# Three casts of q and k moved from GpSimd to ScalarE in a kernel that interleaves sparse attention with a two-layer network

## The chip, the cores and the metric

The kernel runs on one core of a Trainium2 chip. The metric is the device time of one execution in microseconds. The time before is the median of three runs; beside them there is one execution that was recorded by the hardware profiler, and every row of a view comes from that one.

The core's engines each work through their own queue in order: TensorE (PE in the views; its weight loads are PEld), VectorE (DVE), ScalarE (ACT), GpSimd (POOL) and SyncE (SP). A wait at the head of a queue holds everything behind it. SyncE, and in this kernel GpSimd too, issue loads and stores (DMAs).

## The reference

```python
def _attn_ref(q, k, v):                      # 8 batches, 8 heads, 576 positions, 64 wide, float32
    scores = scale * np.matmul(q, k.transpose(0, 1, 3, 2))
    rel = pos[:, None] - pos[None, :]
    mask_local = (rel >= 0) & (rel < 32)                        # heads 0 to 3
    mask_strided = (rel >= 0) & (pos[None, :] % 32 == pos[:, None] % 32)   # heads 4 to 7
    ...                                      # masked softmax over the keys
    return np.matmul(attn, v)

x = attn_out.transpose(0, 2, 1, 3).reshape(B * S, H * D)        # 4608 x 512
h = x @ w_in                                                    # 512 x 2048
g = np.maximum(h, 0.0) + alpha * np.minimum(h, 0.0)
out = g @ w_out                                                 # 2048 x 512
```

## The kernel before

The 4608 rows of x are worked through in nine chunks of 512: a first layer (`hps`, L583), the activation by ScalarE and VectorE (`neg` L591, `gT` L594), and a second layer (`ops`). Attention for a batch's 576 rows must be there before the chunk that uses them, so its pieces are interleaved with the matmuls of the chunk before. Two heads make a pair; a batch has four pairs, two local and two strided. Pair 4 is the first of batch 1, pair 8 the first of batch 2.

For a pair there are these pieces. `T`: q or k of the local heads is transposed by TensorE (L269) and copied from PSUM by ScalarE and VectorE (L207, L209) to `qT` or `kT`. `sc1` and `score_both`: scores by TensorE (L353), exponentials by ScalarE (L367 and L371, in later batches L376 and L382), and a multiplication by the mask, on VectorE for batch 1 (L373) and on GpSimd afterwards (L378, L385). `Pv`: the weighted sum of v (L406), a reciprocal (L413) and the normalisation (L415), both by VectorE. `X`: the result is transposed (L429) and copied to `xT`.

The local q and k of a batch come in as float32 (`load_qk`, L104; tiles `ql`, `kl`) and are cast to float16 by `cast_l` ahead of the transposition. `cast_copy` (L205 to L211) picks the engine: `act` is ScalarE (L207), `dve` VectorE (L209), anything else GpSimd (L211). A cast is one instruction over 128 partitions and 1152 elements. v is loaded by `load_v` (L189, L199) and the strided q and k by `load_d` (L134); GpSimd issues these, and the loads of q and k for batches 1 and 2, and those of `w_out` (L739).

All functions that issue instructions are bound to program order on their engine, so the order in the lists is the order in the queues. The change lies in the list that is run between the first chunk's first layer and the second chunk's. In it `U(kf)` is a step of the first chunk's second layer for three row blocks (three matmuls, L866), `W(i)` two steps for the fourth (L881), `vs` a cast of the strided v by VectorE, `ov` a copy of v's overlapping rows (L209), `G` a transposition of the strided q or k. `loads2` issues the six loads of batch 2 from GpSimd; in the kernel before it also casts batch 2's q and k there. At its end, `U(15)` has its three results copied out by ScalarE, VectorE and ScalarE, which frees the three PSUM banks (`hps`) that the second chunk's first layer uses. After the list come two casts of batch 2's strided v on GpSimd and, on SyncE, the transposing DMAs of its strided q and k and the loads for batch 3.

PSUM banks of the kind `ps`, used by T, Pv, X and parts of the scores, are three, taken in turn: a piece waits until the reader of the third piece before it is done.

Of the kernel before, what the change touches and what calls it, by code (L numbers as in the profile page):

```python
# [32 lines left out]
def kernel(  # L33
# [63 lines left out]
    def load_qk(b, nm):  # L97

        src = q if nm == "q" else k
        t32 = hpool.tile([128, 2, 576], F32, tag=f"{nm}l", bufs=2, name=f"{nm}l")  # L100
        loaded[(b, False, nm)] = t32
        base = src[b, 0:1, 0:1, :]
        eng = nc.gpsimd if b in (1, 2) else nc.sync
        keep(eng.dma_start(t32, bass.AP(  # L104
            tensor=base.tensor, offset=base.offset,
            ap=[[9 * D, 64], [2 * S * D, 2], [S * D, 2], [1, 9 * D]])))
# [24 lines left out]
    def load_d(b):  # L131

        for nm, src in (("q", q), ("k", k)):
            keep(nc.gpsimd.dma_start(  # L134
                qks[nm][0:72], src[b, 4:8, :, :].rearrange("h (p t) d -> p h (t d)", t=8)))
# [24 lines left out]
    def turn_second(nm, pr, eng):  # L160

        dst = (qTs if nm == "q" else kTs)[1].rearrange("r e c -> r (e c)")
        tp = pspool.tile([128, 1024], F16, tag="ps", name="tf")
        for j in range(8):
            keep(nc.tensor.transpose(
                tp[:, 72 * j : 72 * j + 72],
                qks[nm][0:72, 2 * pr + j // 4, 128 * (j % 4) : 128 * (j % 4) + 128], ident[0:72, 0:72]))
        cast_copy(eng, dst[:, 640 * pr : 640 * pr + 640].rearrange("r (j p) -> r j p", p=80)[:, :, 0:72],
                  tp[:, 0:576].rearrange("r (j p) -> r j p", p=72))
# [7 lines left out]
    def cast_l(b, nm, eng="pool"):  # L177
        t16 = hpool.tile([128, 9, 2, 64], F16, tag=f"{nm}l16", bufs=2, name=f"{nm}l16")
        cast_copy(eng, t16, loaded[(b, False, nm)].rearrange("p f (t d) -> p t f d", t=9))
        cast16[(b, False, nm)] = t16  # L180
# [24 lines left out]
    def cast_copy(eng, o, i):  # L205
        if eng == "act":
            keep(nc.scalar.copy(o, i))  # L207
        elif eng == "dve":
            keep(nc.vector.tensor_copy(o, i))  # L209
        else:  # L210
            keep(nc.gpsimd.tensor_copy(o, i))  # L211

    def cast_v(b, pr, eng):

        v16 = vss[b % 2]
        cast_copy(eng, v16[0:72, 2 * pr : 2 * pr + 2, :, 0:64],
                  loaded[b][0:72, 1024 * pr : 1024 * pr + 1024].rearrange(
                      "p (h t d) -> p h t d", h=2, t=8))
        cast16[(b, True, "v")] = v16
# [170 lines left out]
    def pv_piece(P, a):  # L390
        while defer and any(P.et[z][0] is defer_et["et"] for z in P.et):
            defer.pop(0)()
        if P.x16 is None:
            if P.xd and P.strided:
                P.x16 = x16s
            else:
                P.x16 = xpool.tile([128, 1024], F16, tag="x16", name="x16")
        v16 = cast16[(P.b, P.strided, "v")]
        grp = P.pgroups[a]
        r = 72 if P.strided else 128  # L400
        pv = pspool.tile([128, 512], F32, tag="ps", name="pv")
        nb = 2 * len(grp)
        for x in range(nb):
            t, hh = grp[x // 2], x % 2
            et, c = P.et[(t, hh)]
            keep(nc.tensor.matmul(  # L406
                pv[:, 65 * x : 65 * x + 65], et[0:r, c : c + 128],
                v16[0:r, 2 * P.pr + hh, t, :] if P.strided else v16[:, 6 * (2 * P.pr + hh) + t, :],
                start=(x == 0), stop=(x == nb - 1), skip_group_check=True))
        w = P.w  # L410
        rc = rpool.tile([128, 8], F32, tag="rc", name="rc")
        pvv = pv[0:w, 0 : 65 * nb].rearrange("r (c e) -> r c e", e=65)
        keep(nc.vector.reciprocal(rc[0:w, 0:nb], pvv[:, :, 64]))  # L413
        c0 = 128 * grp[0]
        keep(nc.vector.tensor_tensor(  # L415
            P.x16[0:w, c0 : c0 + 64 * nb].rearrange("r (c e) -> r c e", e=64),
            pvv[:, :, 0:64],
            rc[0:w, 0:nb].unsqueeze(2).to_broadcast([w, nb, 64]), op=ALU.mult))
# [7 lines left out]
    def x_piece(P, eng):  # L426
        xp = pspool.tile([128, 1024], F16, tag="ps", name="xp")
        for t in range(P.n):
            keep(nc.tensor.transpose(  # L429
                xp[:, P.w * t : P.w * t + P.w], P.x16[0 : P.w, 128 * t : 128 * t + 128], ident[0 : P.w, 0 : P.w]))  # L430
        for s0, d0, w in spans(P.b):
            o = xT[:, P.hp, d0 : d0 + w]
            if P.strided:
                cast_copy(
                    eng, o.rearrange("r (p t) -> r p t", t=8),
                    xp[:, 0:576].rearrange("r (t p) -> r p t", t=8)[:, s0 // 8 : (s0 + w) // 8, :])
            else:
                cast_copy(eng, o, xp[:, s0 : s0 + w])
# [24 lines left out]
    def T(u, nm):  # L463
        return lambda: transpose_piece(u, nm)
# [4 lines left out]
    def Pv(g, i):  # L469
        return lambda: pv_piece(pairs[g], i)  # L470

    def X(g, eng=None):
        return lambda: x_piece(pairs[g], eng or ("act" if pairs[g].strided else "dve"))
# [332 lines left out]
    def vs(b, pr):  # L806
        return lambda: cast_v(b, pr, "dve")

    def Cl(b, nm):
        return lambda: cast_l(b, nm)  # L810

    def ov(b, eng, c0, c1):
        return lambda: over_v(b, eng, c0, c1)
# [7 lines left out]
    def G(nm, pr):  # L821
        return lambda: turn_second(nm, pr, "act" if nm == "q" else "dve")

    warm(17)
    for fn in [
        F("q", 0), w(1), F("k", 0), w(1), F("k", 1), Sc(2, 0), vs(0, 0), w(1), F("q", 1), Sc(2, 1), alpha, Pv(2, 0),
        Sc(3, 1), vs(0, 1), Cl(0, "q"), Cl(0, "k"), Pv(2, 2), Sc(3, 0), w(1), Pv(3, 2), T(0, "q"), Pv(3, 0), w(1),
        Pv(3, 1), w(1), T(0, "k"), X(3), w(1), Sc(0, 1), Pv(2, 1), Sc(0, 0), Sc(1, 1), ov(0, "dve", 12, 24),
        ov(0, "pool", 0, 12), Pv(0, 1), X(2), Pv(0, 0), Sc(1, 0), Pv(1, 1), L(1), X(0, "act"), Pv(1, 0), L(2), L(3),
        X(1), L(0)]:  # L830
        fn()
# [18 lines left out]
    def loads2():  # L850
        load_qk(2, "q")
        load_qk(2, "k")
        load_v(2, False)
        load_d(2)
        load_v(2, True)
        cast_l(2, "q")
        cast_l(2, "k")

    banks = []

    def U(kf):
        def run():
            if kf == 0:
                banks.extend(phpool.tile([128, 512], F32, tag="hps", name="ops") for _ in range(3))
            for mt in range(3):
                keep(nc.tensor.matmul(  # L866
                    banks[mt], gTs[0][:, kf, 128 * mt : 128 * mt + 128], wout16[:, kf, :],
                    start=(kf == 0), stop=(kf == 15)))
            if kf == 15:
                for mt in range(3):  # L870
                    osb = opool.tile([128, 512], F32, tag="osb", name="osb")
                    cast_copy("dve" if mt == 1 else "act", osb, banks[mt])
                    keep(nc.sync.dma_start(out[128 * mt : 128 * mt + 128, :], osb))
        return run

    def W(i):
        def run():
            if i == 0:
                ops_cur["t"] = pspool.tile([128, 512], F32, tag="ps", name="ops")
            for kf in (2 * i, 2 * i + 1):  # L880
                keep(nc.tensor.matmul(  # L881
                    ops_cur["t"], gTs[0][:, kf, 384:512], wout16[:, kf, :], start=(kf == 0), stop=(kf == 15)))
            if i == 7:
                osb = opool.tile([128, 512], F32, tag="osb", name="osb")
                keep(nc.scalar.copy(osb, ops_cur["t"]))
                keep(nc.sync.dma_start(out[384:512, :], osb))
        return run

    def sc1(g):
        return lambda: score_both(pairs[g], "dve")  # L890

    for fn in [
        U(0), Cl(1, "q"), G("k", 1), vs(1, 0), vs(1, 1), sc1(6), U(1), U(2), sc1(7), U(3), U(4), Cl(1, "k"), loads2,
        Pv(6, 0), Pv(7, 0), Pv(6, 2), U(5), Pv(7, 1), U(6), T(2, "q"), Pv(7, 2), U(7), T(2, "k"), Pv(6, 1), U(8),
        X(7, "dve"), W(0), W(1), sc1(4), U(9), W(2), sc1(5), W(3), ov(1, "dve", 0, 24), W(4), U(10), X(6), U(11),
        Pv(4, 1), W(5), Pv(4, 0), U(12), Pv(5, 1), U(13), U(14), Pv(5, 0), U(15), W(6), X(5), X(4), W(7)]:
        fn()
    for pr in range(2):
        cast_v(2, pr, "pool")
# [63 lines left out]
```

## Time and profile before

| | |
|---|---|
| median of three runs | 302.83 us (302.43 to 303.22) |
| the profiled execution | 303.51 us |
| its span, from the first to the last instruction | 301.5 us |
| TensorE busy | 293.3 us, 97% |
| VectorE busy | 220.8 us, 73% |
| ScalarE busy | 175.5 us, 58% |
| GpSimd busy | 175.8 us, 58% |
| granted TensorE clock | 1.00 |

In a timeline a row gives the start in us from the beginning of the span, the duration in us, the engine, the line of the kernel, the operation, what it writes and reads, the shape, and how many instructions the row merges; brackets give the idle time before it and what ended that. A view of groups gives busy time in us and the mean of one instruction in ns, then the idle time before the group. The row of a window gives, in this order, its length and the busy time of PE, PEld, DVE, ACT and POOL. A view of one line gives minimum, median and maximum duration in ns. A busy share is an average over stages, so the stage in question is read by itself.

### The profile page before, as it was taken

Reading aid. Unit: us, or ns where it says so; the run is one execution under the profiler, and the core shown is the slowest. Engines: PE = TensorE matmul, PEld = TensorE weight load, DVE = VectorE, ACT = ScalarE, POOL = GpSimd, SP = SyncE. Lnnn points to the kernel's source line nnn. Section 1 sums busy time; section 2 is a strip of 40 time slices with the busy share of each in tenths; the row PEclk is TensorE's granted clock in tenths of the full one; section 3 lists DMA queues with packets and bytes.
Section 4 is the critical chain, followed back from the end, with each engine's and each line's share of the span. In section 5 each row is a group of like instructions: output and inputs, shape, how many; then the busy total and the mean of one; then the engine's idle time right before and its main releaser. Section 6 shows DMA issues by size and latency. Waiting matters only on the chain.

```text
span 301.5 us, 6823 instructions
## 1 busy us (share of the span) xinstructions
PE 293.3 (97%) x2683; PEld 181.8 (60%) x2683; DVE 220.8 (73%) x408; ACT 175.5 (58%) x327; POOL 175.8 (58%) x163
## 2 busy tenths in 40 slices
PE   7999989999999999999999999999999999999995
PEld 2664545454555468746874687467745964684484
DVE  4677886768775897589848984888489948936852
ACT  1676734398647775676467646764676356516730
POOL 8362264229959998979897988494653405002300
PEclk9999999999999999999999999999999999999999
DMA  7999999999998979899989998955910140022004
GB/s 179 257 193 202 259 180 252 174 185 334 105 209 159 106 105 81 140 198 140 126 166 188 148 140 170 183 92 91 205 24 20 22 142 0 2 72 70 0 2 140
DMA packets 96976, 41.18 MB, mean 137 GB/s; under 512 B 75360, under 2 KB 93232, under 8 KB 96944
## 3 DMA queue, kind: packets, MB, share of 16 engines
q0 software_dynamic: 51008, 17.77, 57.4%
q1 hardware_dynamic: 45584, 22.32, 34.1%
q10 hardware_dynamic: 352, 0.66, 0.9%
q8 instruction: 21, 0.34, 0.5%
q14 instruction: 11, 0.09, 0.1%
HBM read 38.24 MB, written 9.44 MB: 158 GB/s over the span
## 4 chain that ended last, share of the span: by engine, by line
PE 80%; DVE 10%; ACT 4%; issue 3%; DMA 2%; SPq 0%; ACTq 0%; DVEq 0%
PE hps L583 35%; PE ops L708 25%; PE ops L622 5%; PE pv L406 4%; DVE gT L594 3%; PE ops L866 2%; DVE x L415 2%; PE sp L353 2%; DMA consts<-consts 2%; ACT neg L591 2%; DVE gsum L652 2%; PE xp L429 1%; PE sph L353 1%; PE tp L269 1%; PE ops L881 1%
## 5 line engine op out<-in xcount | busy, mean ns | idle before, releaser
L583 PE MATMUL hps<-xT,win 128*128 128x512 f16 x576 | 131.9, 379 | 0.2 <-ACT xT L452 0.2
L594 DVE SCALAR_TENSOR_TENSOR gT<-neg,oma,hps 128x512 f16<-128x512 f32 x144 | 105.3, 744 | 36.4 <-ACT neg L591 28.4
L591 ACT ACTIVATE neg<-hps 128x512 f32<-128x512 f32 x144 | 85.8, 598 | 35.7 <-PE hps L583 33.7
L583 PEld LDWEIGHTS <-win 128*128 128x128 f16 x576 | 53.7, 98 | 59.2 <-issue 0.5
L652 POOL TENSOR_TENSOR gsum<-gT 128x1024 f16<-128x1024 f16 x14 | 29.7, 2124 | 42.2 <-DVE gT L594 37.2
L378 POOL TENSOR_TENSOR et<-et,consts 128x576 f16<-128x576 f16 (+1 forms) x24 | 34.7, 1447 | 31.7 <-ACT et L376 31.5
L708 PEld LDWEIGHTS <-gsum 128*128 128x128 f16 x448 | 40.9, 98 | 7.3 <-DVE gsum L652 1.9
L708 PE MATMUL ops<-wsum,gsum 128*128 128x256 f16 x328 | 41.6, 273 | 0.3
L708 PEld LDWEIGHTS <-gT 128*128 128x128 f16 x336 | 31.5, 98 | 5.4 <-issue 0.3
L415 DVE TENSOR_TENSOR x<-pv,rc 96x384 f16<-96x384 f32 (+2 forms) x62 | 33.0, 532 | 2.1
L385 POOL TENSOR_TENSOR et<-et,consts 128x576 f16<-128x576 f16 (+1 forms) x24 | 31.4, 1310 | 0.0
L406 PEld LDWEIGHTS <-et 72*128 72x128 f16 (+1 forms) x448 | 23.3, 98 | 13.1 <-issue 1.8
L708 PE MATMUL ops<-wout,gT 128*128 128x256 f16 x224 | 27.9, 273 | 0.1
L376 ACT ACTIVATE et<-sp 128x576 f16<-128x576 f32 (+1 forms) x24 | 15.5, 644 | 17.1 <-PE sp L353 17.1
L413 DVE RECIPROCAL rc<-pv 96x6 f32<-96x6 f32 (+2 forms) x80 | 14.6, 183 | 10.4 <-PE pv L406 10.2
L663 DVE TENSOR_TENSOR osb<-ops,par 128x512 f32<-128x512 f32 (+1 forms) x14 | 9.4, 673 | 16.1 <-PE ops L708 8.2
L382 ACT ACTIVATE et<-sph 128x288 f16<-128x288 f32 (+1 forms) x48 | 18.8, 409 | 0.0
L661 ACT COPY osb<-ops 128x512 f32<-128x512 f32 x14 | 8.2, 585 | 16.8 <-PE ops L708 16.7
L406 PE MATMUL pv<-vs,et 72*128 72x65 f16 x256 | 15.4, 193 | 1.7 <-DVE x L415 0.9
L211 POOL COPY vs<-stv 72x1024 f16<-72x1024 f16 x12 | 13.3, 1116 | 6.3 <-DMA stv<-in_v_dram 6.3
L622 PE MATMUL ops<-wout,gT 128*128 128x512 f16 x64 | 16.4, 379 | 0.0
L725 ACT COPY par<-ops 128x512 f32<-128x512 f32 x13 | 7.6, 585 | 14.1 <-PE ops L708 14.1
(103 smaller groups left out, 334.0 us busy)
## 6 DMA issues: line engine op xcount, KB each, us to landing
out_dram<-osb SPq DMA_DIRECT2D x35, 256.0 KB, 3.8
vl<-in_v_dram POOLq DMA_DIRECT2D x6, 384.0 KB, 9.4
win<-in_moe_w_in_dram POOLq DMA_DIRECT2D x4, 512.0 KB, 17.4
wout<-in_moe_w_out_dram POOLq DMA_DIRECT2D x4, 512.0 KB, 17.9
qsd<-in_q_dram POOLq DMA_DIRECT2D x7, 288.0 KB, 5.8
ksd<-in_k_dram POOLq DMA_DIRECT2D x7, 288.0 KB, 7.9
stv<-in_v_dram POOLq DMA_DIRECT2D x7, 288.0 KB, 8.1
ql<-in_q_dram SPq DMA_DIRECT2D x3, 576.0 KB, 6.9
```

The source lines that it names most:

```text
L376: keep(nc.scalar.activation(ev.rearrange("r (y c) -> r y c", y=2), sp[0:r, :, 0:n], AF.Exp, scale=SCALE))
L378: keep(nc.gpsimd.tensor_tensor(mv, mv, m, op=ALU.mult))
L382: keep(nc.scalar.activation(ev[:, n * y : n * y + n], sps[y][0:r, 0:n], AF.Exp, scale=SCALE))
L385: keep(nc.gpsimd.tensor_tensor(mv, mv, m, op=ALU.mult))
L406: keep(nc.tensor.matmul(pv[:, 65 * x : 65 * x + 65], et[0:r, c : c + 128], v16[0:r, 2 * P.pr + hh, t, :] if P.strided else v16[:, 6 * (2 * ...
L415: keep(nc.vector.tensor_tensor(P.x16[0:w, c0 : c0 + 64 * nb].rearrange("r (c e) -> r c e", e=64), pvv[:, :, 0:64], rc[0:w, 0:nb].unsqueeze ...
L583: keep(nc.tensor.matmul(hps, win16[:, kk, 128 * m : 128 * m + 128], xT[:, kk, c0 : c0 + 512], start=(kk == 2), stop=(kk == 1)))
L591: keep(nc.scalar.activation(neg, hps, AF.Relu, scale=-1.0))
L594: keep(nc.vector.scalar_tensor_tensor(gTs[n][:, m, :], neg, oma[:, m : m + 1], hps, op0=ALU.mult, op1=ALU.add))
L622: keep(nc.tensor.matmul(ops, gTs[n][:, kf, 128 * mt : 128 * mt + 128], wout16[:, kf, :], start=(kf == 0), stop=(kf == 15)))
L652: keep((nc.vector if eng == "dve" else nc.gpsimd).tensor_tensor(gsum[i][:, hs], a, b, op=op))
L708: keep(nc.tensor.matmul(o, lhs(y), rhs(y), start=(first and y == 0), stop=(y == 7), skip_group_check=True))
```

## The change

In the list, the cast of batch 1's local k goes to ScalarE and is moved ahead of `U(3)`, behind `sc1(7)`. Batch 2's two casts leave `loads2`, where they followed the six loads on GpSimd, and go to ScalarE too: q behind `Pv(4, 0)`, k behind `U(12)`. The cast of batch 1's local q stays on GpSimd, as do those of batches 0, 3 and 4. The loads and their order are the same.

```diff
-    def Cl(b, nm):
-        return lambda: cast_l(b, nm)
+    def Cl(b, nm, eng="pool"):
+        return lambda: cast_l(b, nm, eng)
...
         load_v(2, False)
         load_d(2)
         load_v(2, True)
-        cast_l(2, "q")
-        cast_l(2, "k")
...
     for fn in [
-        U(0), Cl(1, "q"), G("k", 1), vs(1, 0), vs(1, 1), sc1(6), U(1), U(2), sc1(7), U(3), U(4), Cl(1, "k"), loads2,
+        U(0), Cl(1, "q"), G("k", 1), vs(1, 0), vs(1, 1), sc1(6), U(1), U(2), sc1(7), Cl(1, "k", "act"), U(3), U(4), loads2,
         Pv(6, 0), Pv(7, 0), Pv(6, 2), U(5), Pv(7, 1), U(6), T(2, "q"), Pv(7, 2), U(7), T(2, "k"), Pv(6, 1), U(8),
         X(7, "dve"), W(0), W(1), sc1(4), U(9), W(2), sc1(5), W(3), ov(1, "dve", 0, 24), W(4), U(10), X(6), U(11),
-        Pv(4, 1), W(5), Pv(4, 0), U(12), Pv(5, 1), U(13), U(14), Pv(5, 0), U(15), W(6), X(5), X(4), W(7)]:
+        Pv(4, 1), W(5), Pv(4, 0), Cl(2, "q", "act"), U(12), Cl(2, "k", "act"), Pv(5, 1), U(13), U(14), Pv(5, 0), U(15), W(6), X(5), X(4), W(7)]:
```

## The prediction, made before the changed kernel had run

> **What bounds the kernel now.** I read the page first, then the stage around the change in the timeline of each engine, then the waits and the windows behind it.
>
> ```profile
> span 301.5 us, 6823 instructions
> PE 293.3 (97%) x2683; PEld 181.8 (60%) x2683; DVE 220.8 (73%) x408; ACT 175.5 (58%) x327; POOL 175.8 (58%) x163
> PE 80%; DVE 10%; ACT 4%; issue 3%; DMA 2%; SPq 0%; ACTq 0%; DVEq 0%
> ```
>
> TensorE is busy for 293.3 of 301.5 us, and the chain of waits lies on it for 80%. So the end moves only if time in which TensorE stands still goes or comes. The places to look at are TensorE's gaps while the second batch is prepared: the casts that move all lie between 39 and 55 us. This is TensorE there (start, duration, then in brackets the idle time and who ended it), with one row of the chain of waits at the end:
>
> ```profile
> 41.99 0.81 PE L866 MATMUL ops<-wout,gT 128*128 128x512 f16 x3
> 43.51 0.36 PE L406 MATMUL pv<-vs,et 72*128 72x65 f16 x6 [0.71 <-DVE x L415]
> ...
> 47.09 0.81 PE L866 MATMUL ops<-wout,gT 128*128 128x512 f16 x3
> 52.75 0.82 PE L866 MATMUL ops<-wout,gT 128*128 128x512 f16 x3
> 54.04 0.36 PE L406 MATMUL pv<-vl,et 128*128 128x65 f16 x6 [0.47 <-DVE vl L209]
> 59.19 2.75 PE L583 MATMUL hps<-xT,win 128*128 128x512 f16 x12
> ```
>
> ```profile
> 43.87 0.65 PE ops L866 x3
> ```
>
> Two gaps are ended by VectorE. Three matmuls of L866 take 0.65 us from issue to issue (the chain's row), so what follows the three at 41.99 could have gone at 42.64 and went at 43.51: 0.87 us late. The same reckoning at 52.75 gives 53.40 against 54.04: 0.64 us late. The row's idle figures, 0.71 and 0.47, are smaller since a matmul's recorded 0.81 holds its drain. Why VectorE is late stands in its own timeline and in GpSimd's:
>
> ```profile
> 41.45 1.31 DVE L373 TENSOR_TENSOR et<-et,consts 72x576 f16<-72x576 f16 x1
> 42.90 0.55 DVE L415 TENSOR_TENSOR x<-pv,rc 72x384 f16<-72x384 f32 x1
> ...
> 51.63 0.46 DVE L373 TENSOR_TENSOR et<-et,consts 128x576 f16<-128x576 f16 x1 [0.58 <-ACT et L367]
> 52.24 1.17 DVE L373 TENSOR_TENSOR et<-et,consts 128x576 f16<-128x576 f16 x1
> 53.44 0.54 DVE L209 COPY vl<-vl 32x1495 f16<-32x1495 f16 x1
> ```
>
> ```profile
> L373 DVE TENSOR_TENSOR et<-et,consts x8: 450/458/1309, 38.8 to 52.2; 72x576 f16<-72x576 f16 x4, 128x576 f16<-128x576 f16 x4
> ```
>
> ```profile
> 39.58 1.15 POOL L211 CAST ql<-ql 128x1152 f16<-128x1152 f32 x1 [7.08 <-DMA ql<-in_q_dram]
> 41.31 1.14 POOL L211 CAST kl<-kl 128x1152 f16<-128x1152 f32 x1 [0.58 <-DMA kl<-in_k_dram]
> 42.39 0.71 POOL L104 DMA_DIRECT2D ql<-in_q_dram  x1
> ...
> 51.63 1.47 POOL L211 CAST ql<-ql 128x1152 f16<-128x1152 f32 x1 [4.22 <-DMA ql<-in_q_dram]
> 53.59 1.40 POOL L211 CAST kl<-kl 128x1152 f16<-128x1152 f32 x1 [0.49 <-DMA kl<-in_k_dram]
> 61.30 2.02 POOL L211 COPY vs<-stv 72x1024 f16<-72x1024 f16 x2 [6.31 <-DMA stv<-in_v_dram]
> 67.65 1.27 POOL L378 TENSOR_TENSOR et<-et,consts 128x576 f16<-128x576 f16 x1 [4.33 <-ACT et L376]
> ```
>
> L373 multiplies the exponentials by the mask; both operands lie in SBUF. Six of its eight calls take about 0.458 us, the median. The other two are the ones that start while GpSimd casts: 41.45 falls into the cast of batch 1's k (41.31 to 42.45) and takes 1.31, 52.24 falls into the cast of batch 2's q (51.63 to 53.10) and takes 1.17. Each ends 0.31 us after the cast does. It also works the other way: the cast at 51.63 met the multiplication at 51.63 and took 1.47 instead of 1.14. So a cast on GpSimd and a mask multiplication on VectorE exclude each other for most of their time, and in these two places TensorE pays. These two casts, and that of batch 2's k, are the ones that leave GpSimd.
>
> **The change, part by part.** The sum is made against the profiled execution, 303.51 us (span 301.5 and 2.01 around it).
>
> Cast of batch 1's k away from GpSimd: the call at 41.45 shrinks from 1.31 to 0.46, so VectorE is 0.85 us earlier in a queue that has no gap up to the L415 at 42.90. That L415 frees the PSUM bank for the weighted sum at 43.51; its end moves from 43.45 to 42.60. TensorE can go at 42.64 by its own queue, and with the 0.06 us that lay between the two it goes at 42.66. Gain 0.85.
>
> Cast of batch 2's q away: the call at 52.24 shrinks from 1.17 to 0.46, by 0.71, and the copy of v's overlap rows (L209, 53.44), for which TensorE waits at 54.04, ends 0.71 earlier. TensorE would be let go at 53.33 and gets there at 53.40. Gain 0.64, the whole gap.
>
> Cast of batch 2's k away (53.59, 1.40 us): GpSimd's next instruction waits for a load until 61.30, the one after it at 67.65 for ScalarE. Nobody waits for this cast. Gain 0.
>
> Three casts onto ScalarE. The trace has no such cast from SBUF there. These are the nearest rows, and ScalarE's timeline where they go:
>
> ```profile
> L452 ACT COPY xT<-xs 128x576 f16<-128x576 f16 x4 | 5.3, 1317 | 0.0
> L207 ACT COPY xT<-xp 128x576 f16<-128x576 f16 x8 | 5.1, 641 | 4.8 <-PE xp L429 4.8
> L452 ACT COPY xT<-xs 128x192 f16<-128x192 f16 x2 | 1.2, 577 | 0.0
> L207 ACT COPY xT<-xp 128x192 f16<-128x192 f16 x2 | 0.7, 340 | 0.0
> ```
>
> ```profile
> 40.73 0.69 ACT L371 ACTIVATE et<-sph 72x288 f16<-72x288 f32 x2
> 44.83 0.75 ACT L207 COPY qT<-tp 128x640 f16<-128x640 f16 x1 [3.41 <-PE tp L269]
> 52.95 0.64 ACT L207 COPY xT<-xp 128x576 f16<-128x576 f16 x1 [0.74 <-PE xp L429]
> 57.57 1.07 ACT L207 COPY osb<-ops 128x512 f32<-128x512 f32 x2 [3.98 <-PE ops L866]
> ```
>
> From PSUM, 192 columns take 340 and 576 take 641 ns: 0.78 ns a column, so 1152 columns are 641 + 576 x 0.784 = 1.09 us. L452 reads SBUF, 577 and 1317 ns: 1.93 ns a column, so 2.43 us. L452 reads single elements a stride of 80 apart; the cast reads runs of 64. I take 1.09 and keep 2.43 as the upper end. Both lie in gaps of ScalarE. Batch 1's k stands behind the exponentials that end at 41.42; it waits for a load that had landed by 41.31. It runs from 41.42 to 42.51, and what is queued behind it, the copy at 44.83, is due at 43.98 after the first gain. Even 2.43 us ends in time, at 43.85. Batch 2's q and k stand behind the copy at 52.95, which ends at 52.74 after that gain: q to 53.83, k (landed at 53.59 in the trace) to 54.92. Behind them are the copies of the finished output at 57.57, due at 56.08 after both gains: 1.16 us to spare, cost 0. At 2.43 us each they end at 57.60, 1.52 late. The first of those copies took some 0.54 us and ended near 58.1, and TensorE needs its bank for the first-layer matmuls from 59.19 on; of the 1.52 some 1.1 is covered, so the upper end costs about 0.45.
>
> Loads. Batch 2's six loads stand behind batch 1's cast of k in GpSimd's queue, so they are issued from 40.73 on (the end of the q cast) instead of 42.39, 1.66 us earlier. Only the moved casts and the copy at 61.30 wait for them, and neither holds the path, so no gain. SyncE's queue gets nothing new: its next loads of q and k, into the buffers that the moved casts read, stand behind the stores of the second layer. The six loads now lie closer to the older load of the third quarter of w_out on the same queue:
>
> ```profile
> L739 POOL DMA_DIRECT2D wout<-in_moe_w_out_dram x1: 753/753/753, 28.0 to 28.0; - x1
> DMA to landing us min/median/max: 17.6/17.6/17.6
> ```
>
> ```profile
> 173.02 2.24 POOL L116 DMA_DIRECT2D kr<-in_k_dram  x3
> 173.56 0.68 DVE L652 TENSOR_TENSOR gsum<-gsum,gT 128x1024 f16<-128x1024 f16 x1
> ...
> 176.15 0.68 DVE L652 TENSOR_TENSOR gsum<-gT 128x1024 f16<-128x1024 f16 x1
> ```
>
> It lands at 45.65, and TensorE first reads it in the three matmuls at 47.09, which move to 46.24: 0.59 us to spare. What was issued earlier on this queue lands earlier here (this load at 45.65, the cast's loads at 51.6 and 53.6 behind it), so I take 0; if its landing slipped by the whole 1.66, that would cost 1.07. And the mask multiplication now runs beside the issue of a load instead of a cast. That costs nothing here: a sum of two SBUF operands (L652) takes 0.68 us beside GpSimd's load issues at 173.02 and 0.68 with GpSimd idle at 176.15.
>
> The Trainium skill (SBUF — State Buffer, "Who interferes with whom") has it that a VectorE instruction with two SBUF inputs and a GpSimd instruction that reads SBUF shut each other out completely, the later one for the whole of the earlier one. By that the call at 41.45 would end at 42.45 + 0.46 = 42.91, where the trace has 42.76, and the one at 52.24 at 53.56, where it has 53.41; the measurement decides, and by the page's rule the gains would be held by TensorE's own queue at 0.87 and 0.64, 1.51 in all.
>
> Sum: -0.85 - 0.64 = -1.49. It stays to the end if TensorE has no slack behind it:
>
> ```profile
> 150.00:200.00 50.00, 49.95 (x479) 31.43 (x477) 37.42 (x70) 31.89 (x61) 41.33 (x36) 1.00 1.24 157
> ```
>
> It has none there, 0.05 us in 50, and GpSimd's masks start at 67.65 upon ScalarE, so they move along. 303.51 - 1.49 = 302.02 for a profiled execution. The median of the runs is 0.68 below the profiled one, so I put it at 302.83 - 1.49 = 301.34, rounded to 301.4. I assume there that the plain runs meet the same two collisions.
>
> **Rivals.**
>
> Half a gain. A cast meets a multiplication only if its load lands in a certain tenth: the k cast began 0.14 us ahead of the multiplication at 41.45. If the load lands 0.2 us later in plain runs, VectorE goes first and there is nothing to save at that place. The plain runs' spread of 0.79 us and their median below the profile speak for it. Against it: if the first collision is missed, VectorE comes earlier to the second place and meets the q cast there anyway, in the copy of v. It leaves 0.64 or 0.85: 302.0 to 302.2.
>
> No gain. What stretched the two calls is not the cast, or the saved time is waited for at a load or a mask later on. For it: GpSimd has no gap for long stretches. Against it: all six calls that met no cast take 0.46, and GpSimd restarts upon ScalarE. It gives 302.8.
>
> Slower: ScalarE's queue held by a load. The k cast brings a load's landing to the head of ScalarE's queue, ahead of the copy of batch 1's transposed q, on which scores and weighted sums hang. On GpSimd a late landing held up nothing of this, only TensorE's later transposes of k. Now each microsecond costs one, from the point where landing plus 1.09 passes 43.98: a landing at 42.89. It came by 41.31, 16.5 us after its issue at 24.80, and the last quarter of w_out took 18.3:
>
> ```profile
> 24.80 0.71 POOL L104 DMA_DIRECT2D kl<-in_k_dram  x1 [1.80 <-DMA win<-in_moe_w_in_dram]
> ```
>
> ```profile
> L739 POOL DMA_DIRECT2D wout<-in_moe_w_out_dram x1: 756/756/756, 31.7 to 31.7; - x1
> DMA to landing us min/median/max: 18.3/18.3/18.3
> ```
>
> With 18.3 us k would land at 43.1 and cost 0.2. Only from 44.4 on is the whole gain of 1.49 gone; with 21 us, at 45.8, the loss is 2.9 and the time 302.83 - 1.49 + 2.9 = 304.2. Against it: the loads land one behind the other, and this one had landed in the trace before ScalarE was free.
>
> **How the numbers follow.** Forecast 0.68, its own range 300.9 (a multiplication that meets the very start of a cast loses 0.85 + 0.14 = 0.99; two of these, 1.98) to 301.9 (1.49 less the 0.45 of slow casts, rounded). Half a gain 0.18, no gain 0.04, slower 0.10. A measurement of this kernel tells about 0.3%, 0.91 us, from no change: faster is below 301.92, slower above 303.74. All of the forecast and a little of the half gain are faster, 0.70; the rest of the half gain and no gain are the same, 0.20; the queue held by a load is slower, 0.10. The range for 8 in 10 goes from 300.9 over the half gain, 302.2, and the 0.2 of a late load on top of it, to 302.4.
>
> **What would show it.** Right: no call of L373 over 0.6 us between 40 and 55 us; the idle 0.71 ahead of the weighted sum at 43.5 and the 0.47 at 54.0 gone; three casts of about 1.1 us on ScalarE, the first starting at the end of an exponential; load issues from 40.7 on; the first-layer matmuls of the second chunk (L583) at 57.7 instead of 59.19; and the span near 300.0. Wrong: ScalarE idle ahead of the k cast with a load as the releaser; a gap of TensorE ahead of the matmuls that first read the third quarter of w_out; output copies that start late behind the casts; or a first half 1.5 us shorter with a gap behind 60 us that takes it back.

## The result, and the profile after

| | before | after |
|---|---|---|
| median | 302.82 us (302.43 to 303.22, 6 runs) | 301.71 us (301.52 to 302.24, 6 runs) |
| profiled execution, span | 303.51, 301.5 us | 301.52, 299.7 us |
| compared again later | 303.20 us (301.62 to 304.34, 22 runs) | 301.73 us (301.35 to 302.18, 12 runs) |

The ratio after to before is 0.9963, 95% interval 0.9949 to 0.9977; in the second comparison 0.9956, 0.9940 to 0.9973. The changed kernel is faster by 1.1 and 1.5 us. Both times lie inside the forecast range, and the two gains on either side of the forecast 1.4.

The page of the changed kernel, TensorE's timeline at the places shown of before, and the view of the mask multiplication's line (L866 has become L864):

```profile
span 299.7 us, 6824 instructions
PE 293.2 (98%) x2683; PEld 181.8 (61%) x2683; DVE 219.1 (73%) x408; ACT 178.6 (60%) x330; POOL 171.9 (57%) x160
```

```profile
41.58 0.81 PE L864 MATMUL ops<-wout,gT 128*128 128x512 f16 x3
42.31 0.36 PE L406 MATMUL pv<-vs,et 72*128 72x65 f16 x6
44.44 0.28 PE L406 MATMUL pv<-vs,et 72*128 72x65 f16 x4 [0.50 <-ACT qT L207]
45.89 0.81 PE L864 MATMUL ops<-wout,gT 128*128 128x512 f16 x3
...
52.21 0.34 PE L406 MATMUL pv<-vl,et 128*128 128x65 f16 x6
57.34 2.75 PE L583 MATMUL hps<-xT,win 128*128 128x512 f16 x12
```

```profile
L373 DVE TENSOR_TENSOR et<-et,consts x8: 447/456/459, 38.4 to 51.0; 72x576 f16<-72x576 f16 x4, 128x576 f16<-128x576 f16 x4
```

TensorE does the same work; what went is idle time. The two brackets of before, 0.71 ahead of the first weighted sum and 0.47 ahead of the last one shown, are gone. All eight mask multiplications take 447 to 459 ns; the longest of before took 1309. The 0.50 at 44.44 was there before, for another reason (ScalarE's copy of the transposed q).

The span is 1.8 us shorter, but not all of that is the change. At the first L866 or L864, ahead of the first moved cast, TensorE is already 0.42 us earlier (36.13 instead of 36.55), so that part belongs to the start of the execution. From there to the second chunk's first L583 it took 22.64 us before (36.55 to 59.19) and takes 21.21 now (36.13 to 57.34): 1.43 us, in two steps. The weighted sum at 43.51 moved by 1.20, 0.79 beyond the 0.41 of its predecessor; the one at 54.04 by 1.83, 0.63 more. The last number stays: the first L583 is 1.85 earlier, the end of the span 1.8.

GpSimd and ScalarE in the same stretch, and the load of w_out's third quarter:

```profile
39.00 1.31 POOL L211 CAST ql<-ql 128x1152 f16<-128x1152 f32 x1 [5.66 <-DMA ql<-in_q_dram]
40.27 0.71 POOL L104 DMA_DIRECT2D ql<-in_q_dram  x1
60.46 2.02 POOL L211 COPY vs<-stv 72x1024 f16<-72x1024 f16 x2 [15.17 <-DMA stv<-in_v_dram]
```

```profile
40.89 1.15 ACT L207 CAST kl<-kl 128x1152 f16<-128x1152 f32 x1
43.63 0.76 ACT L207 COPY qT<-tp 128x640 f16<-128x640 f16 x1 [1.59 <-PE tp L269]
52.29 1.16 ACT L207 CAST ql<-ql 128x1152 f16<-128x1152 f32 x1
53.34 1.15 ACT L207 CAST kl<-kl 128x1152 f16<-128x1152 f32 x1
55.73 1.07 ACT L207 COPY osb<-ops 128x512 f32<-128x512 f32 x2 [1.23 <-PE ops L864]
```

```profile
L739 POOL DMA_DIRECT2D wout<-in_moe_w_out_dram x1: 753/753/753, 28.7 to 28.7; - x1
DMA to landing us min/median/max: 14.6/14.6/14.6
```

The three casts start without idle time and fill gaps; 1.23 us are left ahead of the output copies at 55.73, and 1.59 of the 3.41 ahead of the copy of the transposed q. GpSimd issues the loads from 40.27 on. The load of w_out's third quarter lands at 43.3, long before the 45.89 at which it is read.

### The profile page after: what moved, and what is told of

Same layout as the page of the kernel before. It is cut to its first block, busy times and chain, and to the rows that moved or that the text cites. A ratio compares the mean times of both kernels' runs of the same rounds, so it can differ in the third digit from the quotient of the medians.

```text
span 299.7 us, 6824 instructions
## 1 busy us (share of the span) xinstructions
PE 293.2 (98%) x2683; PEld 181.8 (61%) x2683; DVE 219.1 (73%) x408; ACT 178.6 (60%) x330; POOL 171.9 (57%) x160
## 4 chain that ended last, share of the span: by engine, by line
PE 84%; DVE 7%; ACT 4%; issue 2%; DMA 2%; SPq 0%; DVEq 0%; ACTq 0%
PE hps L583 37%; PE ops L708 24%; PE ops L622 5%; PE pv L406 4%; PE ops L864 3%; DVE gsum L652 2%; DVE gT L594 2%; PE sp L353 2%; DMA consts<-consts 2%; ACT neg L591 1%; PE xp L429 1%; PE sph L353 1%; DVE x L415 1%; PE ops L879 1%; ACT et L382 1%
## 5 line engine op out<-in xcount | busy, mean ns | idle before, releaser
L583 PE MATMUL hps<-xT,win 128*128 128x512 f16 x576 | 131.9, 379 | 0.2 <-ACT xT L452 0.2
L583 PEld LDWEIGHTS <-win 128*128 128x128 f16 x576 | 53.7, 98 | 59.2 <-issue 0.5
L415 DVE TENSOR_TENSOR x<-pv,rc 96x384 f16<-96x384 f32 (+2 forms) x62 | 33.0, 532 | 2.1
```

The source lines that it names most:

```text
L415: keep(nc.vector.tensor_tensor(P.x16[0:w, c0 : c0 + 64 * nb].rearrange("r (c e) -> r c e", e=64), pvv[:, :, 0:64], rc[0:w, 0:nb].unsqueeze ...
L583: keep(nc.tensor.matmul(hps, win16[:, kk, 128 * m : 128 * m + 128], xT[:, kk, c0 : c0 + 512], start=(kk == 2), stop=(kk == 1)))
```

## The experiments

The theory: a cast on GpSimd and VectorE's instruction on SBUF data exclude each other, and TensorE pays. The rivals: the gain comes from the earlier loads; any GpSimd instruction would hold up VectorE; the difference is the start of the execution. The ratios are to the kernel before on the same chip, the times are medians. The kernel before stood at 303.06 beside k1_only, b2_only, memset and q1_too, at 303.02 beside act_more, late_act, late_pool and swap, and at 303.20 beside after_again and swap2. "Stage" is the stretch from the first second-layer matmul to the first L583 of the next chunk, in the profile. The diffs are against the changed kernel unless it is said otherwise, and show only the part of the list that differs.

**One part alone: batch 1's k (k1_only).**

```diff
         load_v(2, True)
+        cast_l(2, "q")
+        cast_l(2, "k")
...
-Pv(4, 0), Cl(2, "q", "act"), U(12), Cl(2, "k", "act"), Pv(5, 1),
+Pv(4, 0), U(12), Pv(5, 1),
```

> Only batch 1's k is cast by ScalarE; batch 2's q and k stay on GpSimd behind the loads. If the collision of a GpSimd cast with the mask multiplication (L373) is the cause: the fourth L373 takes 0.46 us, TensorE gains about 0.8 us at the first gap, and the q cast of batch 2 still meets a VectorE instruction near 50 us, so the second gap stays or grows. Time about 302.0 (301.9 to 302.3). If the earlier loads are the cause: they are as early as in the changed kernel, so the whole gain is there, 301.7, and no second gap. If the movement of start-up is the cause: 302.8.

Measured: 302.53 us, ratio 0.9992 (0.9978 to 1.0006); stage 22.78. No gain that can be told from none, where 302.0 was expected and 302.3 at most. The first gap is gone as expected, but the second has grown threefold (VectorE, GpSimd, TensorE):

```profile
50.83 1.43 DVE L373 TENSOR_TENSOR et<-et,consts 128x576 f16<-128x576 f16 x1 [0.58 <-ACT et L367]
52.66 1.44 DVE L209 COPY vl<-vl 32x1495 f16<-32x1495 f16 x1
```

```profile
50.81 1.14 POOL L211 CAST ql<-ql 128x1152 f16<-128x1152 f32 x1 [5.00 <-DMA ql<-in_q_dram]
52.56 1.15 POOL L211 CAST kl<-kl 128x1152 f16<-128x1152 f32 x1 [0.61 <-DMA kl<-in_k_dram]
```

```profile
54.16 0.35 PE L406 MATMUL pv<-vl,et 128*128 128x65 f16 x6 [1.40 <-DVE vl L209]
```

VectorE comes to batch 1's local pairs earlier and now meets both remaining casts: the seventh L373 the q cast, and the copy of v's overlapping rows the k cast, 1.44 us instead of 0.54. The earlier loads were there in full and brought nothing, so that rival falls. The casts are no separate gains that add up.

**The other part alone: batch 2's q and k (b2_only).**

```diff
-sc1(7), Cl(1, "k", "act"), U(3), U(4), loads2,
+sc1(7), U(3), U(4), Cl(1, "k"), loads2,
```

> Only batch 2's q and k are cast by ScalarE; batch 1's k stays on GpSimd ahead of the loads. Collision: the fourth L373 takes 1.3 us as before, all later ones 0.46, the second gap is gone; gain about 0.63, time 302.2 (302.0 to 302.4). Earlier loads: they are as late as before, so no gain, 302.8, and the second gap stays in the trace.

Measured: 302.30 us, ratio 0.9974 (0.9960 to 0.9988); stage 21.75. The time is as the theory has it, without earlier loads. The collisions differ from the expected one: in this profile, which is that of the slowest of the twelve runs (303.12), two multiplications are slow, neither of them the fourth:

```profile
L373 DVE TENSOR_TENSOR et<-et,consts x8: 443/458/1447, 39.3 to 52.5; 72x576 f16<-72x576 f16 x4, 128x576 f16<-128x576 f16 x4
```

```profile
39.79 1.14 POOL L211 CAST ql<-ql 128x1152 f16<-128x1152 f32 x1 [7.23 <-DMA ql<-in_q_dram]
41.22 1.14 POOL L211 CAST kl<-kl 128x1152 f16<-128x1152 f32 x1 [0.29 <-DMA kl<-in_k_dram]
```

```profile
41.38 1.29 DVE L373 TENSOR_TENSOR et<-et,consts 72x576 f16<-72x576 f16 x1
```

```profile
42.73 0.48 PE L406 MATMUL pv<-vs,et 72*128 72x65 f16 x10 [0.35 <-DVE et L373]
```

The k cast (41.22 to 42.36) met the third L373, which took 1.29 us, and TensorE stood still for 0.35 us behind it; the stage is 0.54 longer than the changed kernel's. The 1447 ns are the second L373: it began at 39.79 together with batch 1's q cast, which stays on GpSimd in every version so far. That one cost nothing, since the third had to wait for ScalarE's exponentials until 41.36 anyway.

**GpSimd occupied, but not reading (memset).**

```diff
-sc1(7), Cl(1, "k", "act"), U(3), U(4), loads2,
+sc1(7), Cl(1, "k", "act"), U(3), U(4), lambda: keep(nc.gpsimd.memset(scr, 0.0)), loads2,
```

> The changed kernel with a memset of an unused tile (128 x 1152, float16) on GpSimd where batch 1's k cast stood, so that GpSimd is occupied beside the third and fourth L373 and the loads are issued late again, but GpSimd reads nothing from SBUF. If what collides is GpSimd's reading: no L373 over 0.6 us, the time stays at 301.7 (301.5 to 302.0). If the earlier loads brought the gain, or if any GpSimd instruction stops VectorE: 302.4 to 302.8, in the second case with an L373 of over 1 us. By the Trainium skill (SBUF - State Buffer, Who interferes with whom) an instruction that only writes does not hold up a VectorE instruction with two SBUF inputs.

Measured: 301.74 us, ratio 0.9966 (0.9954 to 0.9977); stage 21.21, that of the changed kernel to the hundredth.

```profile
40.73 1.05 POOL L892 MEMSET scr<- 128x1152 f16 x1
41.73 0.71 POOL L104 DMA_DIRECT2D ql<-in_q_dram  x1
```

```profile
40.71 1.05 DVE L373 TENSOR_TENSOR et<-et,consts 72x576 f16<-72x576 f16 x2 [1.14 <-ACT et L367]
```

The memset runs from 40.73 to 41.78, across both multiplications of the row below it; the two together take 1.05 us as in the changed kernel. The loads are late again, from 41.73 on, and the gain is there all the same. So it is not the loads, and not GpSimd being busy. The rule of the Trainium skill (SBUF — State Buffer, "Who interferes with whom"), by which a GpSimd instruction that only writes leaves a VectorE instruction with two SBUF inputs alone, agrees with this row. That it is the reading, and not something else in which a cast differs from a memset, is not shown by a run of its own.

**The kernel before, profiled twice more (before_a, before_b).** Unchanged.

> The kernel before once more, for another profile of it. If which VectorE instruction a cast meets depends on when its load happens to land, this profile shows other collisions than the first (a slow third L373, or a slow copy of v, or one collision fewer), with TensorE's idle at the two gaps together between 0.8 and 1.9 us instead of always 1.18. If the collisions are fixed: the fourth and the eighth L373 slow again, 1.3 and 1.2 us, idle 0.7 and 0.5.

> The same as before_a, a second time: whether the sum of the idle at the two gaps differs between executions. Expected from the medians (a gain of 1.1 where the first pair of profiles shows 1.43 in this stage): on average some 0.3 us less than in the first profile.

Measured: one execution each, 303.40 and 303.38 us. First three views of before_a (TensorE, VectorE, GpSimd), then TensorE in before_b:

```profile
42.83 0.36 PE L406 MATMUL pv<-vs,et 72*128 72x65 f16 x6 [0.57 <-DVE x L415]
53.92 0.35 PE L406 MATMUL pv<-vl,et 128*128 128x65 f16 x6 [1.02 <-DVE vl L209]
```

```profile
50.96 1.11 DVE L373 TENSOR_TENSOR et<-et,consts 128x576 f16<-128x576 f16 x1 [0.58 <-ACT et L367]
52.47 1.39 DVE L209 COPY vl<-vl 32x1495 f16<-32x1495 f16 x1
```

```profile
52.31 1.15 POOL L211 CAST kl<-kl 128x1152 f16<-128x1152 f32 x1 [0.55 <-DMA kl<-in_k_dram]
```

```profile
43.17 0.36 PE L406 MATMUL pv<-vs,et 72*128 72x65 f16 x6 [0.57 <-DVE x L415]
53.87 0.36 PE L406 MATMUL pv<-vl,et 128*128 128x65 f16 x6 [0.63 <-DVE vl L209]
```

The two gaps add up to 1.59 and 1.20 us of idle time, against 1.18 in the first profile; the stage took 23.06 and 22.67, against 22.64. The first collision is the k cast with the fourth L373 each time. In the second place it changes. In the first profile the q cast met the eighth L373, and the copy of v was free, 0.54 us. In both of these the q cast met the seventh L373, 1.11 us in before_a and 0.73 in before_b, and the k cast met the copy (52.31 to 53.46 in before_a), which took 1.39 and 1.38. So the price depends on where the loads land. It was not lower than in the first profile, as I had expected of before_b: the stage was 0.42 longer in before_a and 0.03 in before_b.

**The changed kernel again (after_again).**

> The changed kernel again, on the chip of the others, for a narrower interval and as the yardstick of swap2. Ratio to the kernel before 0.9963 (0.9955 to 0.9970), and in the profile no L373 over 0.6 us between 40 and 55 us. If the gain hung on the chip or the day: 0.999 or more.

Measured: 301.73 us, ratio 0.9956 (0.9940 to 0.9973). Stage 21.21 again (36.26 to 57.47), and the longest L373 took 485 ns. This and the profiles above also answer the rival of the start: the stage takes 21.21 us in the three profiles of the changed kernel and the memset, which enter it at 36.13, 36.26 and 36.40. It takes 22.64 to 23.06 in the three of the kernel before, and before_a, the slowest, enters it at 36.00, earlier than any of them.

**How much ScalarE's gap covers (act_more).**

```diff
+    def more():
+        cast_copy("act", scr.rearrange("p (t f d) -> p t f d", t=9, f=2),
+                  loaded[(2, False, "k")].rearrange("p f (t d) -> p t f d", t=9))
...
-Cl(2, "k", "act"), Pv(5, 1),
+Cl(2, "k", "act"), more, more, more, Pv(5, 1),
```

> The changed kernel with three more casts of batch 2's k into an unused tile on ScalarE, behind the two of the change: 3 x 1.15 us more. Theory (ScalarE's gap covers the casts, with 1.2 us idle left and about 1.1 us more until TensorE needs the first PSUM bank): the copies of the finished output start at about 57.9 instead of 55.7, 2.2 late, TensorE loses about 1.1, time 302.8 (302.3 to 303.4). Rival (ScalarE's lateness passes on in full, no cover behind the copies): 303.9. Rival (no cover needed, the copies are not waited for): 301.7.

Measured: 302.84 us, ratio 0.9994 (0.9984 to 1.0004); ScalarE and TensorE:

```profile
54.92 3.52 ACT L207 CAST scr<-kl 128x1152 f16<-128x1152 f32 x3
58.34 1.07 ACT L207 COPY osb<-ops 128x512 f32<-128x512 f32 x2
```

```profile
58.98 1.24 PE L583 MATMUL hps<-xT,win 128*128 128x512 f16 x5 [0.95 <-ACT osb L207]
```

Some 3.4 us of casts more cost 1.1 us: L583 starts 1.55 us after the matmuls ahead of it (57.43), where it took 0.43 in the changed kernel (56.91 to 57.34). About 2.3 are covered, 1.2 by ScalarE's idle time and the rest by the time that TensorE still has until it needs a bank. So the two casts of the change are free, and three more give the gain back.

**The prediction's slower rival, made to happen: the load of batch 1's k lands late.** The same edit in the changed kernel (late_act) and in the kernel before (late_pool):

```diff
-    load_qk(1, "k")
     load_w(2, True)
+    load_qk(1, "k")
```

> The changed kernel with the load of batch 1's k issued behind the third quarter of w_out instead of ahead of it, so that it lands about 4 us later, near 45.5. Theory of the rival of the prediction: ScalarE's queue stands at the k cast until the landing, the copy of the transposed q (43.6) starts about 46.7, 3 us late, and TensorE stands still for about 2.5 to 3 us: 304.2 to 304.9. If ScalarE's place for the cast does not matter: as late_pool.

> The kernel before with the same later load of batch 1's k. GpSimd waits for it instead; held up are the loads of batch 2 behind it (by 4 us) and TensorE's transposes of k. Theory: the q side goes on, TensorE's transposes of k come about 0.5 to 1 us late, the first collision is gone since the cast comes later, but another VectorE instruction may meet it; 302.3 to 303.8, less than late_act by 1 us or more. If the later loads of batch 2 are waited for: over 304.

Measured: 306.25 us, ratio 1.0110 (1.0082 to 1.0138), on ScalarE; 304.48 us, ratio 1.0046 (1.0030 to 1.0062), on GpSimd. First ScalarE, TensorE and two windows in late_act, then GpSimd and TensorE in late_pool:

```profile
46.34 1.15 ACT L207 CAST kl<-kl 128x1152 f16<-128x1152 f32 x1 [4.55 <-DMA kl<-in_k_dram]
```

```profile
43.94 0.79 PE L269 MATMUL tp<-consts,ql 128*128 128x128 f16 x9
48.19 0.38 PE L406 MATMUL pv<-vs,et 72*128 72x65 f16 x4 [3.46 <-ACT qT L207]
48.38 1.47 PE L864 MATMUL ops<-wout,gT 128*128 128x512 f16 x3
```

```profile
47.00:48.00 1.00, 0.00 (x0) 0.00 (x0) 0.00 (x0) 1.00 (x2) 0.30 (x1) 0.83 1.51 187
48.00:49.00 1.00, 0.81 (x6) 0.47 (x6) 0.36 (x2) 0.14 (x1) 0.00 (x0) 0.50 1.12 267
```

```profile
45.65 1.14 POOL L211 CAST kl<-kl 128x1152 f16<-128x1152 f32 x1 [4.99 <-DMA kl<-in_k_dram]
```

```profile
46.84 0.68 PE L269 MATMUL tp<-consts,kl 128*128 128x128 f16 x9 [1.13 <-POOL kl L211]
55.17 0.36 PE L406 MATMUL pv<-vl,et 128*128 128x65 f16 x6 [1.15 <-DVE vl L209]
```

The mechanism is as told: ScalarE waits 4.55 us for the load with the copy of the transposed q behind it, and TensorE stands still for 3.46 us instead of 0.50; on GpSimd the same landing costs 1.13 at the transposes of k. Both are dearer than expected. In late_pool the casts of batch 2 met the seventh L373 (1.14 us) and v's copy (1.49 us), and TensorE stood still for 1.15 us there. Its time is above the 304 that the expectation tied to batch 2's later loads being waited for, but batch 2's q cast begins at 51.73, right behind the last load issue, with no idle time. In late_act the clock dropped: the window from 48 to 49 has a granted clock of 0.50 (the third number from the end), the next two as well, the one after them 0.96, and three second-layer matmuls take 1.47 us instead of 0.81. TensorE stood still for 2.96 us more, and some 1.4 us were lost in the 2.9 us that it worked at half the clock. Together these are 4.3 of the 4.5 us between 306.25 and 301.71; the stage is 4.2 longer (25.43).

**Batch 1's q on ScalarE too (q1_too).**

```diff
-U(0), Cl(1, "q"), G("k", 1),
+U(0), G("k", 1),
...
-sc1(7), Cl(1, "k", "act"), U(3),
+sc1(7), Cl(1, "q", "act"), Cl(1, "k", "act"), U(3),
```

> The changed kernel with batch 1's q cast moved to ScalarE as well, ahead of the k cast. In the profile of the changed kernel the q cast on GpSimd ends at 40.31, just ahead of the L373 at 40.44, so the profiled span gains nothing. If plain executions meet this cast now and then: median lower by 0.1 to 0.4, 301.3 to 301.6, and a narrower spread. If not: 301.7. Against it: two casts in a row end at about 43.2 on ScalarE, 0.4 ahead of the copy of the transposed q at 43.63; if q's transposition comes late, 302 or more.

Measured: 301.71 us, ratio 0.9961 (0.9947 to 0.9975): no gain beyond the change that can be seen, though the interval reaches 0.4 us to either side and so does not exclude the gain of 0.1 to 0.4. The stage took 21.22, as in the changed kernel. (The whole span of this profile cannot be compared: its granted clock was 0.87 between 10 and 36 us, ahead of the stage.) The q cast that stayed on GpSimd can cost something: in act_more it ran from 40.27 to 41.41, and the third L373 took 1011 ns.

```profile
L373 DVE TENSOR_TENSOR et<-et,consts x8: 444/457/1011, 38.7 to 51.6; 72x576 f16<-72x576 f16 x4, 128x576 f16<-128x576 f16 x4
```

```profile
41.35 0.90 PE L406 MATMUL pv<-vs,et 72*128 72x65 f16 x16
```

The sixteen matmuls behind it take 0.90 us, where the changed kernel's take 0.65 (at 41.09), so TensorE lost 0.25 us to this collision. It adds to the 1.1 us that the three casts cost in act_more's stage (22.58).

**The gap that is left.** A step of the second layer is moved ahead of the weighted sum at 44.44 (swap), then a second one ahead of the next (swap2):

```diff
-T(2, "q"), Pv(7, 2), U(7), T(2, "k"), Pv(6, 1), U(8),    # changed kernel
+T(2, "q"), U(7), Pv(7, 2), T(2, "k"), Pv(6, 1), U(8),    # swap
+T(2, "q"), U(7), Pv(7, 2), T(2, "k"), U(8), Pv(6, 1),    # swap2
```

> The changed kernel with a second-layer step (three matmuls) moved ahead of the weighted sum for which TensorE still stands still 0.50 us (44.44). The gap is filled, but the next weighted sum then follows 0.65 us sooner and waits for its PSUM bank: of 0.50 some 0.15 to 0.3 stays as gain, 301.4 to 301.6. If the wait merely moves in full: 301.7.

> The reordering of swap, and the next second-layer step as well moved ahead of the weighted sum that then waited 0.22 us for its bank. If the bank is free in the meantime, the 0.22 go too: 0.0007 below swap, 0.993 to 0.994 of the kernel before, 301.1 to 301.3. If the transposition behind it (X) now waits for a bank instead: as swap, 301.4.

```profile
43.50 0.81 PE L864 MATMUL ops<-wout,gT 128*128 128x512 f16 x3
44.17 0.28 PE L406 MATMUL pv<-vs,et 72*128 72x65 f16 x4
44.29 0.67 PE L269 MATMUL tp<-consts,kl 128*128 128x128 f16 x9
45.19 0.36 PE L406 MATMUL pv<-vs,et 72*128 72x65 f16 x6 [0.22 <-DVE x L415]
```

Measured: swap 301.42 us, ratio 0.9945 (0.9931 to 0.9960), stage 20.88; swap2 301.39 us, ratio 0.9947 (0.9928 to 0.9965), stage 20.80. Of the 0.50 us 0.33 went, and 0.22 came up at the next weighted sum, as expected. The second move brought 0.08 in the stage instead of 0.22, and nothing in the median that can be told from swap: TensorE reaches the next scores 0.40 us sooner after the stage's start and loses 0.33 in them (the matmuls into `sph` take 0.62 us instead of 0.29). The trace does not name what they wait for. Both stand 0.3 us below the changed kernel's 301.7 and are the best versions that were run; their intervals to the kernel before overlap with its own.

## Why the prediction was right

The cause was right. In the pair of profiles the gaps close by what the two stretched multiplications had cost, in the places named, and a GpSimd that only writes does no harm. The second chunk's first L583 was expected at 57.7 and stands at 57.34, or 57.76 with the 0.42 of the earlier start added. That the sum came out so near is partly luck, as the step on batch 2's k shows below.

One reading needs a limit: "all six calls that met no cast take 0.46". Two of the six overlap a cast, those at 39.27 (q cast from 39.58) and at 51.63 (q cast from the same moment). They took 0.46 because they had begun before the cast or with it; at 51.63 it was the cast that was held.

First gain: 0.85 expected, 0.79 measured. The recorded 1.31 us of the blocked multiplication overlapped what came behind it more than a free one does (42.90 for the L415 after an end at 42.76, now 41.70 after 41.49), and TensorE still waits some 0.08 us for the bank.

Second gain: 0.64 expected, 0.63 measured.

Casts on ScalarE: 1.09 taken, 1.15 measured; the 2.43 of the strided reads was the wrong end by far. Cost 0, as expected; the cover behind them, reckoned at 1.16 plus 1.1, is confirmed by three casts more.

Loads and w_out: no cost, and 2.6 us to spare instead of 0.59, since the load landed earlier this time.

Batch 2's k, "nobody waits for this cast, gain 0": true of the first profile alone. In before_a, before_b, k1_only and late_pool it is this cast that the copy of v waits for. The step read one execution as if its collisions were fixed; that the change moves this cast as well is probably why the gain held although the collisions vary. The same holds for the rival with half a gain: with batch 1's k alone on ScalarE nothing measurable was left of the gain, since VectorE, come earlier, meets the next cast; that was its own argument against, and it decided. The copy of v is held by a cast as it said there, though by that of k and not of q: 1.38 to 1.49 us in these four profiles instead of 0.54.

From the profile to the median: 1.49 was carried over, on the assumption that plain runs meet the same two collisions. The profiles meet varying ones. The two comparisons give 1.1 and 1.5; the interval of the first reaches from 0.7 to 1.5 us. That the kernel before spreads over 2.7 us in the second comparison and the changed one over 0.8 fits collisions that vary. Two of the 22 took 301.62 and 301.64 us, no longer than the changed kernel. But the three profiled executions of before (303.51, 303.40, 303.38) all lie above the medians, so that the short runs are those without collisions is not shown. Whether the first gain is the lower one by chance or by milder collisions stays open; the three profiles of before show none that were milder.

The slower rival needed a landing past 44.4. Its mechanism is real, and a microsecond there costs one: in late_act the copy of the transposed q starts 2.98 us later after the stage's start than in the changed kernel, and TensorE 2.96. Its price was set too low all the same: it left out the clock.

## What to carry to other kernels

Where a VectorE instruction on SBUF data (here a product of two SBUF operands and a copy from SBUF to SBUF) is now and then two or three times as long as its fellows, look at what GpSimd does at that moment; moving that work to an engine with a gap can shorten the kernel although GpSimd itself has time to spare. Move all the casts of such a stretch: with one of them gone, the queue moves up into the next. Batch 1's k alone brought nothing measurable, batch 2's two alone 0.26%, all three 0.37 and 0.44%. And a cast that waits for a load belongs on a queue where little stands behind it, or where the load is certain to be there.

## What the runs showed of the hardware that I had not expected

In late_act TensorE's granted clock fell to 0.50 while TensorE stood still for 3.46 us; in late_pool it did not fall in 1.13. The 0.83 of the window from 47 to 48 puts the fall at about 47.66, an estimate: 2.9 us after the end of the matmuls at 43.94 (44.73). The Trainium skill (TensorE: Matmul & The Clock Gate, "Part 1: The HAM clock gate") gives an idle window of about 3.4 us for this; here the clock fell some 0.5 us sooner, and the measurement decides.

A VectorE instruction that was held by a cast ended at a fixed distance behind it: a multiplication by the mask 0.31 us after the cast's end in the profiles of before, k1_only, b2_only and act_more, though alone it takes 0.46, and the copy of v 0.40 after it in before_a, before_b, k1_only and late_pool, though alone it takes 0.54.

A cast of 1152 float32 elements from SBUF on ScalarE (1.15 us) took about as long as an undisturbed one on GpSimd (1.14), and came near the 1.09 that the rate of reads from PSUM gives, not the 2.43 of the strided copies.
